# Decay attention in blocks of 64 tokens instead of 128, with a state formed in the middle of each chunk

## The chip, the core and the metric

The kernel runs on one core of a Trainium2 chip. The metric is the device time of one execution in microseconds (us), as the median of repeated runs. Five engines matter here: TensorE (PE, matrix multiplies, which read their weights by a separate load instruction, PEld), VectorE (DVE), ScalarE (ACT), GpSimd (POOL) and SyncE (SP), which issues the DMA transfers. TensorE writes to PSUM, which has eight banks; every tile called "bank" is one of them.

## The reference

Two stages follow each other. The first is linear attention with an exponential decay per head, the second a feed-forward network with a squared ReLU.

```python
B, H, S, D = 4, 8, 768, 64           # q, k, v; lam: one decay per head
# attention, in blocks of 64 tokens:
intra = einsum('bhic,bhjc->bhij', qb, kb) * Dmask      # lam ** (i - j), i >= j
intra = einsum('bhij,bhjd->bhid', intra, vb)
inter = einsum('bhid,bhde->bhie', qb * lam_pow, kv_state)
out   = intra + inter
kv_state = lam_block * kv_state + einsum('bhsd,bhse->bhde', kb * rev_pow, vb)
...
# feed-forward: x is (3072, 512), w_in (512, 2048), w_out (2048, 512)
h = maximum(x @ w_in, 0.0)
result = h * h @ w_out
```

The size of the block is a choice of whoever computes this: a longer block does more of the work as masked scores between tokens, a shorter one does more of it through the state.

## The kernel before, in words

**Tiles and chunks.** The 3072 tokens are cut into 24 chunks of `C = 128` tokens, six for each of four batches. A tile is three chunks (`NT = 3`, 384 columns), so there are eight tiles. For each tile the attention of its three chunks fills the tile's `x` (as a high part `xh` and a low part `xl`), and the feed-forward part then runs 16 steps (`NF`) over the hidden units. A step is `mm1` (L485: 12 multiplies with 384 columns into one bank), the squared ReLU on ACT and DVE (L499 to L506), and `mm2` (L491, L492, L494: 9 multiplies with 512 columns into three banks). From the third tile on, two steps are taken together.

**Attention.** The first chunk of each batch is done by `unit_first`; the change leaves it alone. The 20 others are done by `unit`. A unit has two parts on TensorE:

- `front` (L431): `scores` (L344) multiplies keys with queries, 16 matmuls, then `update` (L350) multiplies decayed keys with values to give what the chunk adds to the state, 16 matmuls. Both write the same two banks `sc`. The last chunk of a batch needs no new state and has only `scores`.
- `both` (L449): the old state is multiplied with the queries (L452, 8 matmuls), and `values` (L358) multiplies the masked scores with the weighted values, 16 matmuls, both into the two banks `ys`.

All these matmuls are 64 by 64 with float32 operands; four of them at a time sit in the four quarters of the array (`QUARTERS`). In `scores` and `values` a chunk is split into two halves of `TW = 64` tokens. Half `j = 0` of the keys meets all 128 queries, half `j = 1` only the 64 later ones, so half of these matmuls have 128 columns and half have 64. The old state meets all 128 queries at once.

**Between the two parts** DVE works. `begin_` (L436) multiplies the scores in `sc` with the mask (L437, two operations over 384 elements), adds the update in `sc` to the old state (L442, two operations over 128 elements, tile `hold`), and scales the new state (L445). After `both`, `back` (L455) copies on ACT (L456), adds and scales on DVE (L457, L458), and splits into `xh` (ACT, L460) and `xl` (DVE, L461).

**What sets the order.** A planner written in Python (`Plan.order`) places every operation on its engine by guessed durations, keys (due times), dependencies and free buffers; its order is what each engine then runs. Guessed durations change the order, not the work. Where the planner expects TensorE to be idle before 45 us it puts in dummy multiplies (`filler`, L230). The first two units, chunks (0,1) and (1,1), are planned alone: `front` and `both` are separate operations of TensorE. The other 18 are fused by `turn_over` (L558): one operation of TensorE holds the `front` of one unit and, behind it, the `both` of the unit before. A fused operation therefore comes about every 20 to 27 us between the steps of the feed-forward part.

**Weights** of the feed-forward part arrive as 64-bit floats and are converted on ACT and DVE (L290 to L300) during roughly the first 110 us.

Of the kernel before, what the change touches and what calls it, by code (L numbers as in the profile page):

```python
# [14 lines left out]
ALU = mybir.AluOpType  # L15
PSUM = bass.MemoryType.PSUM

B, H, S, D = 4, 8, 768, 64
DM, DFF = 512, 2048
P = 128  # L20
C = 128
# [5 lines left out]
R = 2  # L27
# [119 lines left out]
TW = C // 2  # L147
SPAN = C + TW
QUARTERS = ((0, 0), (1, 1), (0, 1), (1, 0))
# [7 lines left out]

TWO, BOTH = 2, 9.0

EDGE = 0.15  # L160

WEIGHTS0, WKEY1, WKEY2, KLATE, ULATE = -9.0, 7.0, 2.0, 6.0, 16.0

LEAD = 0.6


@with_exitstack
def kernel(ctx: ExitStack, tc: tile.TileContext, pn, lamx, w, out):
    nc = tc.nc
# [29 lines left out]
    mask = const.tile([P, 2 * P], F32, name="mask")[:, 0:SPAN]  # L199
# [5 lines left out]
    def at(b):  # L205
        return tiles[b.kind][b.slot]
# [49 lines left out]
    def dm():  # L256
# [6 lines left out]
        out=wd2.rearrange("p (r e) -> p r e", r=R), in0=wdec.rearrange("p (r j e) -> p r j e", r=R, j=2)[:, :, 0],  # L263
        in1=lam[:, 0:H].rearrange("p (r j e) -> p r j e", r=R, j=2)[:, :, 0], op=ALU.mult), [o_pow])
    o = plan.op("PE", 1.0, -12, spread, [o_wb], [wb, dps])
    o_dm = [plan.op("DVE", 0.22, -12, lambda h=h: nc.vector.scalar_tensor_tensor(  # L266
        out=dm()[:, h, 0:C], in0=at(dps)[:, h * C:h * C + C], scalar=wd2[:, h:h + 1], in1=mask[:, 0:C], op0=ALU.mult, op1=ALU.mult), [o, o_wd2], [dps, decay]) for h in range(NS)]
# [3 lines left out]
        out=rdec.rearrange("p (r v) i -> p r v i", v=2)[:, :, v], in0=at(rps[v])[:, 0:2 * C].rearrange("p (r i) -> p r i", r=R),  # L271
        in1=lam[:, H:H + NP].rearrange("p (r v) -> p r v", v=2)[:, :, v].unsqueeze(2).broadcast_to([P, R, C]), op=ALU.mult),
# [40 lines left out]
    half = lambda h: slice(h * 64, h * 64 + 64)  # L313
# [7 lines left out]
    def k_(t, r, s, j):  # L321
        return at(t)[half(r), 0, s * C + j * TW:s * C + j * TW + TW]

    def q_(t, r, s, i=0):
        return at(t)[half(r), 1, s * C + i:s * C + C]

    def head(r, j, e):
        return (r * 2 + j) * 2 + e

    def heads(a):  # L330
        return a.rearrange("p (h d) -> p h d", h=H)
# [7 lines left out]
    def scores(t, sc):  # L339
        for e in range(2):  # L340
            for j in range(2):
                for r, v in QUARTERS:
                    o_ = at(sc[r])[half(v), e * SPAN + j * C:e * SPAN + j * C + C - j * TW]
                    nc.tensor.matmul(o_, k_(t, r, 2 * v + e, j), q_(t, r, 2 * v + e, j * TW), start=e == j == 0, stop=True, skip_group_check=True)  # L344

    def update(kt, vd, u, col, start):
        for e in range(2):
            for j in range(2):
                for v, r in QUARTERS:
                    nc.tensor.matmul(  # L350
                        at(u[v])[half(r), col + e * D:col + e * D + D], kt()[half(v), head(r, j, e)],
                        heads(at(vd))[half(v), head(r, j, e)], start=start and e == j == 0, stop=True, skip_group_check=True)

    def values(v_, s1, ys, start):
        for r in range(R):
            for j in range(2):
                for v, e in QUARTERS:
                    nc.tensor.matmul(  # L358
                        at(ys[v])[half(e), (2 + r) * C + j * TW:(3 + r) * C], v_()[half(v), head(r, j, e)], at(s1[r])[half(v), e, j * C:j * C + C - j * TW],
                        start=start and r == j == 0, stop=j == 1, skip_group_check=True)  # L360

    def y_(ys, v):
        return at(ys[v])[:, 2 * C:4 * C].rearrange("p (r i) -> p r i", r=R)
# [50 lines left out]
    def unit(b, c, x, col, key, span, behind=None, vd_act=False, alone=False):  # L414

        t, tv, vd, s1, xr = Buf("in"), Buf("in"), Buf("half"), [Buf("s1") for _ in range(R)], Buf("half")
        sc, ys = [Buf("bank") for _ in range(2)], [Buf("bank") for _ in range(2)]
        last = c == NC_ - 1
        old, o_old = state[b]

        def add(eng, dur, dk, fn, deps, bufs, name=None):
            o = plan.op(eng, dur, key + dk * span, fn, deps, bufs)
            return in_turn(name, o) if name else o

        i = CHUNKS.index((b, c))
        l = load(1.7, key - 8, lambda: at(t), pn[i, 0], [t], "load", behind)
        loadv = load(1.7, key - 7.9, lambda: at(tv), pn[i, 1], [tv], "load", behind)
        v_, kt = (lambda n=n: heads(at(tv)[:, n]) for n in range(2))
        o_vd = add("ACT" if vd_act else "DVE", 2.2 if vd_act else 0.6, 0, lambda: weighted(v_, vd, vd_act), [loadv, o_pow], [tv, vd], "vd")

        def front():  # L431
            scores(t, sc)
            if not last:
                update(kt, vd, sc, 2 * SPAN, False)

        def begin_(o_sc):  # L436
            so = [add("DVE", 0.45, 0.2, lambda r=r: nc.vector.tensor_tensor(  # L437
                out=at(s1[r]), in0=at(sc[r])[:, 0:2 * SPAN].rearrange("p (e i) -> p e i", e=2),
                in1=mask.unsqueeze(1).broadcast_to([P, 2, SPAN]), op=ALU.mult), [o_sc], [sc[r], s1[r]], f"s1{r}") for r in range(R)]
            if not last:  # L440
                new = Buf("hold")
                os_ = [add("DVE", 0.22, 0.3, lambda v=v: nc.vector.tensor_tensor(  # L442
                    out=at(new)[:, 2 * v:2 * v + 2], in0=at(sc[v])[:, 2 * SPAN:2 * SPAN + 2 * D].rearrange("p (e d) -> p e d", e=2), in1=at(old)[:, 2 * v:2 * v + 2], op=ALU.add),
                    [o_sc] + o_old, [sc[v], new, old]) for v in range(2)]
                state[b] = (new, [add("DVE", 0.35, 0.3, lambda: nc.vector.tensor_tensor(  # L445
                    out=at(new), in0=at(new), in1=lc.unsqueeze(2).broadcast_to([P, NS, D]), op=ALU.mult), os_, [new])])
            return so

        def both():  # L449
            for v in range(2):  # L450
                for r, e in QUARTERS:
                    nc.tensor.matmul(at(ys[r])[half(e), v * C:v * C + C], at(old)[half(r), 2 * v + e], q_(t, r, 2 * v + e), start=v == 0, stop=True, skip_group_check=True)  # L452
            values(lambda: heads(at(vd)), s1, ys, False)

        def back(o_y):  # L455
            oc = [add("ACT", 0.33, 1, lambda r=r: nc.scalar.copy(x4(xr)[:, 2 * r:2 * r + 2], at(ys[r])[:, 0:2 * C].rearrange("p (v i) -> p v i", v=2)), [o_y], [ys[r], xr], f"yi{r}") for r in range(R)]  # L456
            oa = [add("DVE", 0.36, 1, lambda v=v: nc.vector.tensor_tensor(out=by_v(x4(xr), v), in0=y_(ys, v), in1=by_v(x4(xr), v), op=ALU.add), oc, [ys[v], xr]) for v in range(2)]  # L457
            xo = add("DVE", 0.6, 1, lambda: nc.vector.tensor_tensor(out=x4(xr), in0=x4(xr), in1=rdec, op=ALU.mult), oa + o_rdec, [xr])  # L458
            cs = slice(col, col + C)
            oh = add("ACT", 0.55, 1, lambda: nc.scalar.copy(at(x)[0][:, :, cs], x4(xr)), [xo], [xr, x])  # L460
            ol = add("DVE", 0.6, 1, lambda: nc.vector.tensor_tensor(  # L461
                out=at(x)[1][:, :, cs], in0=x4(xr), in1=at(x)[0][:, :, cs], op=ALU.subtract), [oh], [xr, x])
            return [oh, ol]

        dep_f, buf_f, dur_f = [l] + ([] if last else [o_vd, loadv]), [t] + sc + ([] if last else [tv, vd]), 0.7 if last else 1.2
        buf_v, dur_v = ys + [t, vd, x, old] + s1, 1.15
        if alone:
            o_sc = add("PE", dur_f + EDGE, 0, front, dep_f, buf_f, "sc")
            so = begin_(o_sc)
            return back(add("PE", dur_v + EDGE, 1, both, so + [o_vd] + o_old, buf_v, "y"))  # L470
        return dict(key=key, front=Part(dur_f, front, dep_f, buf_f), begin=begin_, values=Part(dur_v, both, [o_vd] + o_old, buf_v), back=back)

    last_mm, steps = {}, {}
# [77 lines left out]
    for f in range(NF):  # L551
        t = FIRST + f * SLOW_STEP
# [35 lines left out]
    def attention(ti):  # L588
        for j, (b, c) in enumerate(TILES[ti]):
            u = unit(b, c, xs[ti], j * C, begin[ti - 1] + (j - LEAD) * NF / NT * per[ti - 1], 4.0, steps[0, BEHIND] if ti == 2 else None)  # L590
            u["last"] = begin[ti - 1] + (NT - LEAD) * NF / NT * per[ti - 1]
            so = turn_over(u)
            pending.append((u, so, done_x[ti]))

    for ti, cs in enumerate(TILES):
        x, ready = xs[ti], done_x[ti]
# [7 lines left out]
        os_ = [Buf("bank") for _ in cs]  # L604
# [44 lines left out]
```

## Time and profile before

| What | Value |
|---|---|
| median of three runs | 611.14 us (611.11 to 611.68) |
| the profiled execution's own time | 611.9 us |
| span of the profiled execution | 610.2 us |
| TensorE matmul records | 5268 |
| VectorE busy over the span | 310.0 us |
| ScalarE busy over the span | 224.8 us |

The profile comes from one execution. A row of a group names line, engine, operation, tiles (output and inputs), shape and count, then busy time in us and the mean of one in ns. A row of the timeline gives start and length in us; neighbouring instructions of one line are merged, with their count behind an x. Every float32 matmul of the program appears as two matmul records: L452 stands in 20 units with 8 matmuls each, and has 320 records. Matmuls overlap one another in the engine, so the length of one record is not the time that it costs; what it costs is read from the starts of successive records or groups.

### The profile page before, as it was taken

To read this page: it belongs to the slowest core of one execution; us is meant where nothing else is said; L and a number is where in the kernel's file an instruction comes from. 1 tells how busy PE (TensorE), PEld (TensorE's weight loads), DVE (VectorE), ACT (ScalarE), POOL (GpSimd) and SP (SyncE) were. 2 spreads that over 40 slices of the span, in tenths; PEclk is the share of its full clock that TensorE was granted. 3 is DMA by queue.
4 is the path that set the end of the run, shared out by engine and by line. 5 is a ranking of instruction groups with operands and counts; after the bars stand their busy time and mean duration, and the time that the engine had idled before them with its cause. 6 is when DMAs were issued, how large, how long until landed. Compare 5 with 4: busy or idle time off the path is not lost.

```text
span 610.2 us, 12175 instructions
## 1 busy us (share of the span) xinstructions
PE 603.4 (99%) x5268; PEld 544.0 (89%) x5268; DVE 310.0 (51%) x623; ACT 224.8 (37%) x477; POOL 4.6 (1%) x14
## 2 busy tenths in 40 slices
PE   8999999999999999999999999999999999999997
PEld 7889999898999898898998998989989899899996
DVE  6899999854334434444353453353443443332222
ACT  6767777542432232232222332322323232232221
POOL 3000000000000000000000000000000000000000
PEclk9999999999999999999999999999999999999999
DMA  8865555532112202112021320130210100010001
GB/s 289 292 217 173 188 193 186 190 127 104 35 53 70 74 32 71 52 36 71 0 71 56 100 70 1 36 110 13 70 48 23 54 1 0 1 37 18 0 1 52
DMA packets 15749, 49.02 MB, mean 80 GB/s; under 512 B 1872, under 2 KB 1872, under 8 KB 15696
## 3 DMA queue, kind: packets, MB, share of 16 engines
q1 hardware_dynamic: 15696, 48.25, 23.6%
q8 instruction: 41, 0.67, 0.5%
q14 instruction: 12, 0.10, 0.1%
HBM read 41.95 MB, written 6.29 MB: 79 GB/s over the span
## 4 chain that ended last, share of the span: by engine, by line
PE 96%; DMA 2%; DVE 1%; ACT 0%; issue 0%; SPq 0%; DVEq 0%
PE bank L485 44%; PE bank L491 15%; PE bank L492 14%; PE bank L494 14%; PE bank L344 3%; PE bank L358 3%; DMA in<-w 2%; PE bank L452 2%; PE bank L350 1%; PE bank L230 1%; DVE in L266 0%; ACT m L290 0%; DVE xl L461 0%; DVE m L540 0%; DVE m L295 0%
## 5 line engine op out<-in xcount | busy, mean ns | idle before, releaser
L491 PE MATMUL bank<-woh,gh 128*128 128x512 f32 x384 | 151.7, 395 | 0.1
L505 DVE TENSOR_TENSOR g<-g 128x384 f32<-128x384 f32 x96 | 53.6, 558 | 190.4 <-ACT gh L504 190.4
L492 PE MATMUL bank<-wol,gh 128*128 128x512 f32 x384 | 149.9, 390 | 0.0
L499 ACT ACTIVATE g<-bank 128x384 f32<-128x384 f32 x128 | 62.8, 491 | 191.2 <-PE bank L485 190.7
L485 PE MATMUL bank<-xh,wih 128*128 128x384 f32 x512 | 110.5, 338 | 0.0
L485 PE MATMUL bank<-xh,wil 128*128 128x384 f32 x512 | 109.6, 336 | 0.0
L485 PE MATMUL bank<-xl,wih 128*128 128x384 f32 x512 | 109.5, 336 | 0.0
L494 PE MATMUL bank<-woh,gl 128*128 128x512 f32 x384 | 100.6, 390 | 0.0
L485 PEld LDWEIGHTS bank<-xh,wih 128*128 128x128 f32 x512 | 91.1, 188 | 4.6
L485 PEld LDWEIGHTS bank<-xh,wil 128*128 128x128 f32 x512 | 90.6, 188 | 0.0
L485 PEld LDWEIGHTS bank<-xl,wih 128*128 128x128 f32 x512 | 90.4, 188 | 0.0
L506 DVE TENSOR_TENSOR gl<-g,gh 128x384 fp32r<-128x384 f32 x128 | 71.4, 558 | 30.7 <-ACT gh L502 21.6
L491 PEld LDWEIGHTS bank<-woh,gh 128*128 128x128 f32 x384 | 72.1, 188 | 14.6 <-ACT gh L502 0.6
L494 PEld LDWEIGHTS bank<-woh,gl 128*128 128x128 f32 x384 | 71.9, 188 | 14.7
L492 PEld LDWEIGHTS bank<-wol,gh 128*128 128x128 f32 x384 | 72.1, 188 | 12.9
L504 ACT ACTIVATE gh<-g 128x384 fp32r<-128x384 f32 x96 | 50.4, 525 | 63.7 <-PE bank L492 61.8
L456 ACT COPY half<-bank 128x256 f32<-128x256 f32 x40 | 12.9, 375 | 50.3 <-PE bank L358 50.3
L290 ACT ACTIVATE m<-in 128x512 f32<-128x512 f32 x32 | 21.5, 675 | 14.2 <-DVE wol L300 6.2
L344 PEld LDWEIGHTS bank<-in 64*64 64x64 f32 x768 | 18.5, 133 | 7.6 <-issue 6.9
L437 DVE TENSOR_TENSOR s<-bank,mask 128x384 f32<-128x384 f32 x40 | 20.6, 552 | 9.1 <-PE bank L350 8.2
L540 DVE COPY ob<-bank 128x512 f32<-128x512 f32 x15 | 10.3, 688 | 23.9 <-PE bank L494 21.1
L297 DVE SCALAR_TENSOR_TENSOR m<-in,m 128x512 uint32<-128x512 uint32 x32 | 22.1, 690 | 0.0
(59 smaller groups left out, 378.5 us busy)
## 6 DMA issues: line engine op xcount, KB each, us to landing
in<-pn SPq DMA_DIRECT2D x44, 512.0 KB, 4.6
in<-w SPq DMA_DIRECT2D x32, 512.0 KB, 3.7
out<-ob SPq DMA_DIRECT2D x23, 256.0 KB, 2.1
half<-pn SPq DMA_DIRECT2D x8, 256.0 KB, 5.5
out<-m SPq DMA_DIRECT2D x1, 256.0 KB, 2.0
g<-lamx SPq DMA_DIRECT2D x1, 8.0 KB, 1.6
```

The costliest lines, as they stand in the source:

```text
L290: o = add("ACT", 0.55, lambda: nc.scalar.activation(at(m), words(1).bitcast(F32), AF.Abs), [o], [st, m])
L297: o = add("DVE", 0.6, lambda: nc.vector.scalar_tensor_tensor(out=bits(), in0=words(0), scalar=29, in1=bits(), op0=ALU.logical_shift_right, ...
L344: nc.tensor.matmul(o_, k_(t, r, 2 * v + e, j), q_(t, r, 2 * v + e, j * TW), start=e == j == 0, stop=True, skip_group_check=True)
L437: so = [add("DVE", 0.45, 0.2, lambda r=r: nc.vector.tensor_tensor(out=at(s1[r]), in0=at(sc[r])[:, 0:2 * SPAN].rearrange("p (e i) -> p e i" ...
L485: nc.tensor.matmul(at(h)[:, 0:N], wt[:, cc, :], xt[:, cc, :], start=k == 0, stop=k == 3 * NCC - 1)
L491: nc.tensor.matmul(at(os_[j]), at(gh)[:, sl], woh[f], start=f == 0, stop=False)
L492: nc.tensor.matmul(at(os_[j]), at(gh)[:, sl], wol[f], start=False, stop=False)
L494: nc.tensor.matmul(at(os_[j]), at(gl)[:, sl], woh[f], start=False, stop=f == NF - 1)
L499: orr = plan.op("ACT", 0.45, key - (AHEAD if ti < 2 else 0), lambda: nc.scalar.activation(at(g), at(h)[:, 0:N], AF.Relu), [o1], [h, turn_, g])
L504: ogh = plan.op("ACT", 0.47, key, lambda: nc.scalar.activation(at(gh), at(g), AF.Square), [orr], [g, gh])
L505: og = plan.op("DVE", 0.48, key, lambda: nc.vector.tensor_tensor(out=at(g), in0=at(g), in1=at(g), op=ALU.mult), [orr, ogh], [g])
L506: ogl = plan.op("DVE", 0.48, key - (AHEAD if ti < 2 else 0), lambda: nc.vector.tensor_tensor(out=at(gl), in0=at(g), in1=at(gh), op=ALU.sub ...
```

## The change

Each chunk of a unit is now treated as two blocks of 64 tokens. A second state, `mid`, is formed for the middle of the chunk: old state plus what the first half adds. The later half of the queries then meets `mid` instead of meeting the first half's keys directly.

- `scores64`: 16 matmuls, all with 64 columns, each half of the keys with its own half of the queries.
- `update64`: 8 matmuls for each half of the chunk, kept apart in the bank. Other chunks have both halves (16 matmuls, as before); the last chunk of a batch, which had none, has the first half (8).
- `old64`: 16 matmuls with 64 columns, the first half of the queries with `old`, the second with `mid`.
- `values64`: 16 matmuls, all with 64 columns.
- On DVE the mask covers 256 elements in each of two operations; two more operations of 128 elements form `mid` in every unit; the new state is then formed from `mid`.
- `front` of a last chunk now also waits for the weighted values and their load, as the other chunks' did.
- The planner's guesses change with it: `EDGE` from 0.15 to 0.2, the mask operation from 0.45 to `S64 = 0.36`, `front` from 1.2 to 1.0 (last chunk 0.7 to 0.75), `both` from 1.15 to 1.0.

```diff
-EDGE = 0.15
+EDGE = 0.2
...
+S64 = 0.36
...
+    def scores64(t, sc):
+        for e in range(2):
+            for j in range(2):
+                for r, v in QUARTERS:
+                    i = (e * 2 + j) * TW
+                    nc.tensor.matmul(at(sc[r])[half(v), i:i + TW], k_(t, r, 2 * v + e, j), q_(t, r, 2 * v + e, j * TW, j * TW + TW), start=e == j == 0, stop=True, skip_group_check=True)
+
+    def update64(kt, vd, u, col, blocks):
+        for j in range(blocks):
+            for e in range(2):
+                for v, r in QUARTERS:
+                    i = col + (j * 2 + e) * D
+                    nc.tensor.matmul(
+                        at(u[v])[half(r), i:i + D], kt()[half(v), head(r, j, e)],
+                        heads(at(vd))[half(v), head(r, j, e)], start=False, stop=True, skip_group_check=True)
+
+    def old64(t, states, ys):
+        for v in range(2):
+            for j in range(2):
+                for r, e in QUARTERS:
+                    i = v * C + j * TW
+                    nc.tensor.matmul(at(ys[r])[half(e), i:i + TW], at(states[j])[half(r), 2 * v + e], q_(t, r, 2 * v + e, j * TW, j * TW + TW), start=v == j == 0, stop=True, skip_group_check=True)
+
+    def values64(vd, s1, ys):
+        for r in range(R):
+            for j in range(2):
+                for v, e in QUARTERS:
+                    i = (2 + r) * C + j * TW
+                    nc.tensor.matmul(
+                        at(ys[v])[half(e), i:i + TW], heads(at(vd))[half(v), head(r, j, e)], s64(s1[r])[half(v), e * 2 + j],
+                        start=False, stop=True, skip_group_check=True)
...
         def front():
-            scores(t, sc)
-            if not last:
-                update(kt, vd, sc, 2 * SPAN, False)
+            scores64(t, sc)
+            update64(kt, vd, sc, 4 * TW, 1 if last else 2)
 
         def begin_(o_sc):
-            so = [add("DVE", 0.45, 0.2, lambda r=r: nc.vector.tensor_tensor(
-                out=at(s1[r]), in0=at(sc[r])[:, 0:2 * SPAN].rearrange("p (e i) -> p e i", e=2),
-                in1=mask.unsqueeze(1).broadcast_to([P, 2, SPAN]), op=ALU.mult), [o_sc], [sc[r], s1[r]], f"s1{r}") for r in range(R)]
+            so = [add("DVE", S64, 0.2, lambda r=r: nc.vector.tensor_tensor(
+                out=s64(s1[r]), in0=at(sc[r])[:, 0:4 * TW].rearrange("p (n i) -> p n i", n=4),
+                in1=mask[:, 0:TW].unsqueeze(1).broadcast_to([P, 4, TW]), op=ALU.mult), [o_sc], [sc[r], s1[r]], f"s1{r}") for r in range(R)]
...
+            om = [add("DVE", 0.22, 0.2, lambda v=v: plus(mid, old, 0, v), [o_sc] + o_old, [sc[v], mid, old]) for v in range(2)]
             if not last:
                 new = Buf("hold")
...
+                os_ = [add("DVE", 0.22, 0.3, lambda v=v: plus(new, mid, 1, v), [om[v]], [sc[v], new, mid]) for v in range(2)]
...
-            return so
+            return so + om
 
         def both():
-            for v in range(2):
-                for r, e in QUARTERS:
-                    nc.tensor.matmul(at(ys[r])[half(e), v * C:v * C + C], at(old)[half(r), 2 * v + e], q_(t, r, 2 * v + e), start=v == 0, stop=True, skip_group_check=True)
-            values(lambda: heads(at(vd)), s1, ys, False)
+            old64(t, states, ys)
+            values64(vd, s1, ys)
...
-        dep_f, buf_f, dur_f = [l] + ([] if last else [o_vd, loadv]), [t] + sc + ([] if last else [tv, vd]), 0.7 if last else 1.2
-        buf_v, dur_v = ys + [t, vd, x, old] + s1, 1.15
+        dep_f, buf_f, dur_f = [l, o_vd, loadv], [t] + sc + [tv, vd], 0.75 if last else 1.0
+        buf_v, dur_v = ys + [t, vd, x, old, mid] + s1, 1.0
```

More of the change, by code (lines that the diff above doesn't have):

```diff
@@ L322, in k_, with q_ @@
         return at(t)[half(r), 0, s * C + j * TW:s * C + j * TW + TW]
-    def q_(t, r, s, i=0):
-        return at(t)[half(r), 1, s * C + i:s * C + C]
+    def q_(t, r, s, i=0, end=C):
+        return at(t)[half(r), 1, s * C + i:s * C + end]
     def head(r, j, e):
@@ L360, in values, with s64 @@
                         start=start and r == j == 0, stop=j == 1, skip_group_check=True)
+    def scores64(t, sc):
[26 more added lines that the diff above has]
+                        start=False, stop=True, skip_group_check=True)
+    def s64(b):
+        return at(b).rearrange("p e i -> p (e i)")[:, 0:4 * TW].rearrange("p (n i) -> p n i", n=4)
     def y_(ys, v):
@@ L429, in unit, with plus @@
         o_vd = add("ACT" if vd_act else "DVE", 2.2 if vd_act else 0.6, 0, lambda: weighted(v_, vd, vd_act), [loadv, o_pow], [tv, vd], "vd")
+        mid = Buf("hold")
+        states = (old, mid)
         def front():
-            scores(t, sc)
-            if not last:
-                update(kt, vd, sc, 2 * SPAN, False)
+            scores64(t, sc)
+            update64(kt, vd, sc, 4 * TW, 1 if last else 2)
         def begin_(o_sc):
-            so = [add("DVE", 0.45, 0.2, lambda r=r: nc.vector.tensor_tensor(
-                out=at(s1[r]), in0=at(sc[r])[:, 0:2 * SPAN].rearrange("p (e i) -> p e i", e=2),
-                in1=mask.unsqueeze(1).broadcast_to([P, 2, SPAN]), op=ALU.mult), [o_sc], [sc[r], s1[r]], f"s1{r}") for r in range(R)]
+            so = [add("DVE", S64, 0.2, lambda r=r: nc.vector.tensor_tensor(
+                out=s64(s1[r]), in0=at(sc[r])[:, 0:4 * TW].rearrange("p (n i) -> p n i", n=4),
+                in1=mask[:, 0:TW].unsqueeze(1).broadcast_to([P, 4, TW]), op=ALU.mult), [o_sc], [sc[r], s1[r]], f"s1{r}") for r in range(R)]
+            def plus(to, base, j, v):
+                i = (4 + 2 * j) * TW
+                return nc.vector.tensor_tensor(
+                    out=at(to)[:, 2 * v:2 * v + 2], in0=at(sc[v])[:, i:i + 2 * D].rearrange("p (e d) -> p e d", e=2), in1=at(base)[:, 2 * v:2 * v + 2], op=ALU.add)
+            om = [add("DVE", 0.22, 0.2, lambda v=v: plus(mid, old, 0, v), [o_sc] + o_old, [sc[v], mid, old]) for v in range(2)]
@@ L440, in begin_ @@
             if not last:
                 new = Buf("hold")
-                os_ = [add("DVE", 0.22, 0.3, lambda v=v: nc.vector.tensor_tensor(
-                    out=at(new)[:, 2 * v:2 * v + 2], in0=at(sc[v])[:, 2 * SPAN:2 * SPAN + 2 * D].rearrange("p (e d) -> p e d", e=2), in1=at(old)[:, 2 * v:2 * v + 2], op=ALU.add),
-                    [o_sc] + o_old, [sc[v], new, old]) for v in range(2)]
+                os_ = [add("DVE", 0.22, 0.3, lambda v=v: plus(new, mid, 1, v), [om[v]], [sc[v], new, mid]) for v in range(2)]
```

## The prediction

> **What bounds the kernel now.** I read the page first, then the busy time by stage, then who waited for whom on TensorE, and last the timeline of single attention blocks.
>
> ```profile
> span 610.2 us, 12175 instructions
> PE 603.4 (99%) x5268; PEld 544.0 (89%) x5268; DVE 310.0 (51%) x623; ACT 224.8 (37%) x477; POOL 4.6 (1%) x14
> PEclk9999999999999999999999999999999999999999
> PE 96%; DMA 2%; DVE 1%; ACT 0%; issue 0%; SPq 0%; DVEq 0%
> ```
>
> TensorE is busy throughout and carries 96% of the chain that ended last, at full granted clock. A busy share says little by itself, because overlapping matmuls count as busy, so I look at it by stage:
>
> ```profile
> core 0: us, PE busy (x) PEld busy (x) DVE busy (x) ACT busy (x) POOL busy (x), PEclk, DMA share, GB/s
> 0.00:16.00 16.00, 13.94 (x262) 11.04 (x262) 10.38 (x29) 9.96 (x34) 4.59 (x14) 1.00 0.84 292
> 16.00:44.00 28.00, 27.49 (x497) 22.93 (x497) 25.64 (x60) 20.71 (x55) 0.00 (x0) 1.00 0.80 268
> 44.00:110.00 66.00, 66.00 (x339) 60.52 (x339) 65.80 (x136) 48.65 (x93) 0.00 (x0) 1.00 0.55 179
> 110.00:527.00 417.00, 417.00 (x3770) 378.07 (x3772) 183.41 (x358) 125.07 (x256) 0.00 (x0) 1.00 0.17 56
> ```
>
> There are three stages. Up to 44 us TensorE has gaps and dummy multiplies and DVE is 92% busy (25.64 of 28). From 44 to 110 us both are full: DVE converts weights, TensorE has a backlog of feed-forward steps. From 110 us on DVE is 44% busy and TensorE has no gap. The waits of TensorE, over the whole span and then from 44 us on (an empty list under its heading), say the same:
>
> ```profile
> PE bank L230 <- DVE ob L213: 1.5, 1, 1.5
> PE bank L358 <- DVE s L391: 0.5, 1, 0.5
> PE bank L452 <- DVE hold L442: 0.4, 1, 0.4
> ```
>
> ```profile
> engine line waited for: us in total, times, longest us
> ```
>
> So behind 44 us every microsecond that TensorE is spared is a microsecond of the result, as long as nothing new makes it wait. All 18 fused units lie there; only the two planned alone lie in the start.
>
> **What a quarter-set of matmuls costs.** Here is a fused block of a normal chunk, and one whose front belongs to the last chunk of a batch. The starts in the first column matter, not the lengths in the second.
>
> ```profile
> 204.67 0.90 PE L344 MATMUL bank<-in 64*64 64x128 f32 x32
> 205.39 0.65 PE L350 MATMUL bank<-half,in 64*64 64x64 f32 x32
> 205.86 0.62 PE L452 MATMUL bank<-in,hold 64*64 64x128 f32 x16
> 206.29 0.85 PE L358 MATMUL bank<-s,half 64*64 64x128 f32 x32
> 207.07 0.50 PE L491 MATMUL bank<-woh,gh 128*128 128x512 f32 x1
> ```
>
> ```profile
> 259.42 0.90 PE L344 MATMUL bank<-in 64*64 64x128 f32 x32
> 260.14 0.62 PE L452 MATMUL bank<-in,hold 64*64 64x128 f32 x16
> 260.57 0.85 PE L358 MATMUL bank<-s,half 64*64 64x128 f32 x32
> 261.35 0.97 PE L485 MATMUL bank<-xh,wih 128*128 128x384 f32 x4
> ```
>
> ```profile
> L344 PE MATMUL bank<-in 64*64 64x128 f32 x384 | 19.1, 282 | 0.0
> L344 PE MATMUL bank<-in 64*64 64x64 f32 x384 | 14.5, 217 | 0.0
> L452 PE MATMUL bank<-in,hold 64*64 64x128 f32 x320 | 12.7, 272 | 0.4 <-DVE hold L442 0.4
> L350 PE MATMUL bank<-half,in 64*64 64x64 f32 x512 | 10.5, 218 | 0.0
> ```
>
> The update is pure 64 columns: 32 records from 205.39 to 205.86, 0.47 us, or eight sets of four at 58 ns (14.7 ns a record). The old-state product is pure 128 columns: 16 records from 205.86 to 206.29, 0.43 to 0.44 us, four sets at 109 ns. The scores are half and half by the form rows, so four sets of each: 4 x 109 + 4 x 58 = 668 ns, and 0.72 us were taken, so 0.05 us is the entry to the block. The values likewise take 0.78 us, 668 ns plus 0.11 us for the way back to the 128-row multiplies. Two prices and two edges explain the whole block, 2.40 us (204.67 to 207.07). A set costs nearly in proportion to its columns, with about 5 ns on top.
>
> **The change on TensorE, part by part**, at 58 ns a set and with the edges unchanged:
> - scores64: eight sets, 464 ns against 668: -0.20 us.
> - update64: normal chunk, the same eight sets: 0. Last chunk, four new sets: +0.23.
> - old64: eight sets, 464 ns against 4 x 109 = 436: +0.03. Twice the matmuls with half the columns each cost only the fixed part.
> - values64: 464 ns against 668: -0.20, so -0.18 for the two parts of `both` together.
>
> A normal unit so saves 0.38 us; a last one 0.20 - 0.23 + 0.18 = 0.15 us. Of the 18 fused units four are last chunks and 14 are not: 14 x 0.38 + 4 x 0.15 = 5.9 us. By the stage table all of it is on the path.
>
> The Trainium skill has a rule against this. The page "TensorE: Matmul & The Clock Gate", section "Wait — 56ns, not 53.3ns?" in Part 1, states that matmuls never start closer than about 25 ns however few columns they have; by that a set of four would cost 100 ns, a normal block 32 x 100 ns and the edges, 3.4 us, and the result would come out some 18 us slower (an estimate from that page). The trace disagrees where it can be read: the update's 32 records start 14.7 ns apart on average, four quarters at work together.
>
> **DVE in a fused block.** Two operations in a row overlap too, so occupancy comes from pairs:
>
> ```profile
> 33.59 0.76 DVE L457 TENSOR_TENSOR half<-bank,half 128x256 f32<-128x256 f32 x2 [0.90 <-ACT half L456]
> 35.80 1.02 DVE L437 TENSOR_TENSOR s<-bank,mask 128x384 f32<-128x384 f32 x2
> 37.76 0.48 DVE L442 TENSOR_TENSOR hold<-bank,hold 128x128 f32<-128x128 f32 x2
> L437 DVE TENSOR_TENSOR s<-bank,mask 128x384 f32<-128x384 f32 x40 | 20.6, 552 | 9.1 <-PE bank L350 8.2
> L442 DVE TENSOR_TENSOR hold<-bank,hold 128x128 f32<-128x128 f32 x32 | 8.7, 283 | 0.0
> L457 DVE TENSOR_TENSOR half<-bank,half 128x256 f32<-128x256 f32 x40 | 15.1, 419 | 13.0 <-ACT half L456 13.0
> ```
>
> A pair's length less one mean is the step: 0.47 us for 384 elements, 0.34 for 256, 0.20 for 128. The mask operations shrink from 384 to 256 elements (-0.26 us a unit), the two that form `mid` add 0.40: +0.14 us a unit. DVE is 44% busy behind 110 us, so it pays this from idle time. Its results are needed a whole unit later by TensorE, since `both` runs one block after its `front`. What does follow soon is the release of the `sc` banks, which now takes one pair more:
>
> ```profile
> 209.34 0.28 DVE L442 TENSOR_TENSOR hold<-bank,hold 128x128 f32<-128x128 f32 x1
> 211.29 0.86 PE L485 MATMUL bank<-xh,wih 128*128 128x384 f32 x4
> ```
>
> The last reader of `sc` ends at 209.62, 1.67 us before the next multiply that opens a bank. With 0.14 us more, or 0.40 if the shorter masks help nothing, 1.2 us are left. I cost it at nothing; without that cover it would be at most 0.40 us a block. In a last chunk `sc` is newly held until `mid` is formed, and its front newly waits for the weighted values; their load is placed a unit ahead, and the planner puts other steps first if they are late.
>
> **The start.** The two units planned alone run before 44 us, where DVE leads.
>
> ```profile
> 38.10 0.75 PE L452 MATMUL bank<-in,hold 64*64 64x128 f32 x13 [0.37 <-DVE hold L442]
> 39.55 1.99 PE L230 MATMUL bank<-ob 128*128 128x256 f32 x8
> 43.83 0.69 DVE L461 TENSOR_TENSOR xl<-half,xh 128x512 fp32r<-128x512 f32 x1
> 44.27 0.86 PE L485 MATMUL bank<-xh,wih 128*128 128x384 f32 x4
> ```
>
> TensorE's endless stretch begins at 44.27, when the second tile's `x` is complete (`xl` at 44.52); just before, it ran dummies for want of DVE. If DVE's occupancy decides, the start moves by 2 x 0.14 = +0.3 us; if the chain through a unit decides, by 2 x (0.14 - 0.38) = -0.5; if TensorE's own work, by -0.8. The new wait for `mid` stands at L452's place in that chain, with the values and the next feed-forward step queued behind it on TensorE. The changed guesses also let the planner reorder DVE's queue, and one conversion operation in the wrong place costs the 0.69 us of a 512-element row such as L461. I take 0, between the ends, since DVE's +0.3 is nearest to what the stage table shows and one unit's shorter chain offsets it; for the range -0.8 to +2 (three misplaced operations).
>
> **Sum.** -5.9 + 0. The profiled execution's own time of 611.9 us (span 610.2 and 1.7 around it) becomes 606.0; the median of the runs, 611.14, lies 0.8 lower and becomes 605.2 us.
>
> **Rivals.**
> 1. *TensorE is limited by the number of records, not by columns* (slower). The update is 32 records in a row; the new block is 128 at that pace, longer than anything the trace holds. Should a queue in front of the array be drained by the short run and refilled more slowly, the block would go at the refill's pace. The block before averages 2.40 us / 112 records = 21.4 ns. At that pace a normal block takes 128 x 21.4 ns = 2.74 us (+0.34, 13 of them), one with a last front, 80 records before (259.42 to 261.35, 1.93 us) and 112 now, 2.40 (+0.47, four), the final values-only block +0.1: +6.4 us, 617.5. It decides from about 18 ns a record, where the 2240 new records cost as much as the old blocks did. Against it: the update comes behind 32 scores records already faster than the block's mean, and shows no slowing. The floor of 25 ns in the Trainium skill (the same page and section) would be its extreme form.
> 2. *New waits in the block.* If banks, or DVE behind a longer queue, hold TensorE for 0.33 us in each of 18 blocks, nothing remains: 611. The margin of 1.67 us and an idle DVE speak against it.
> 3. *The start slips* by 2 to 4 us through another order of DVE's queue: 607.2 to 609.2. The planner is sensitive, and a conversion chain takes several 0.69 us pieces; but the dummies show slack of its own on TensorE only.
> 4. *The change does part of what it says*: sustained sets cost 65 ns instead of 58. 560 sets in the fused blocks x 7 ns = 3.9 us given back: 609.
>
> **How the numbers follow.** Forecast 0.78; rival 1 0.07; rival 2 0.05; rival 3 0.06; rival 4 0.04. The forecast's own range is 604.4 (start at -0.8) to 607.2 (start at +2); to hold 8 in 10 it reaches a little into rivals 3 and 4: 604.2 to 607.8. A measurement of this kernel can tell about 0.2%, 1.2 us, from no change. Faster by more: forecast and rivals 3 and 4, 0.88; within it: rival 2, 0.05; slower: rival 1, 0.07.
>
> **What would show it.** Right: in the profile after, a normal fused block takes 2.02 us from its first record to the next feed-forward multiply, one with a last front 1.79, with sets 58 ns apart in all four groups; TensorE's list of waits behind the start stays empty; matmul records rise by 384 to 5652 less or more a few dummies. Wrong: a block that lengthens after its first 30 to 60 records (rival 1), entries of TensorE waiting for DVE or banks (rival 2), or a first uninterrupted feed-forward step well after 44.3 us (rival 3).

## The result: 606.19 us, and the profile after

The change takes 606.19 us (median of five runs, 605.93 to 608.62) beside 611.56 us for the kernel before (five runs). The ratio is 0.9922, with a 95% interval from 0.9909 to 0.9935. The forecast was 605.2 us, with a range of 604.2 to 607.8. The profiled execution took 605.93 us, where 606.0 was worked out for it. In a later comparison the same kernel took 606.28 us (four runs) beside 611.52 us (eleven): 0.9916, interval 0.9900 to 0.9931.

The page of the profile after shows the same picture as before, 6.0 us shorter, with 388 matmul records more (384 from the change and two more dummy multiplies, which have two records each):

```profile
span 604.2 us, 12989 instructions
PE 598.2 (99%) x5656; PEld 538.5 (89%) x5656; DVE 312.0 (52%) x663; ACT 225.0 (37%) x477; POOL 4.7 (1%) x14
PE 94%; DMA 3%; ACT 1%; DVE 1%; issue 0%; SPq 0%; ACTq 0%; DVEq 0%
```

The busy time by stage (last stage cut where the attention ends) still has TensorE without a gap behind 44 us, and DVE at 45% behind 110 us:

```profile
44.00:110.00 66.00, 66.00 (x340) 60.45 (x339) 65.92 (x137) 49.15 (x93) 0.00 (x0) 1.00 0.57 181
110.00:521.00 411.00, 411.00 (x4091) 372.10 (x4093) 184.42 (x392) 124.78 (x256) 0.00 (x0) 1.00 0.17 57
```

Whom TensorE waited for: two entries in all, both in the start. From 44.4 us on the list is empty.

```profile
PE bank L232 <- DVE ob L215: 1.5, 1, 1.5
PE bank L385 <- DVE hold L482: 0.3, 1, 0.3
```

The timeline of TensorE shows the fused block of a normal chunk, and one with a last chunk's front (L369 scores, L376 update, L385 old state, L392 values):

```profile
203.42 0.69 PE L369 MATMUL bank<-in 64*64 64x64 f32 x32
203.94 0.65 PE L376 MATMUL bank<-half,in 64*64 64x64 f32 x32
204.40 0.65 PE L385 MATMUL bank<-in,hold 64*64 64x64 f32 x32
204.87 0.65 PE L392 MATMUL bank<-s,half 64*64 64x64 f32 x32
205.45 0.50 PE L533 MATMUL bank<-woh,gh 128*128 128x512 f32 x1
...
257.42 0.69 PE L369 MATMUL bank<-in 64*64 64x64 f32 x32
257.94 0.41 PE L376 MATMUL bank<-half,in 64*64 64x64 f32 x16
258.17 0.65 PE L385 MATMUL bank<-in,hold 64*64 64x64 f32 x32
258.64 0.65 PE L392 MATMUL bank<-s,half 64*64 64x64 f32 x32
259.21 0.45 PE L527 MATMUL bank<-xh,wih 128*128 128x384 f32 x1
```

Read the starts again: 0.52, 0.46, 0.47 and 0.58 us, 2.03 in all where 2.40 stood. The block with a last front takes 1.79 us where 1.93 stood.

For the whole, take the stretch from the second tile's first feed-forward multiply to the last multiply of the kernel. The first pair of rows is the kernel before (its start stands in the prediction already), the second the change:

```profile
605.59 0.39 PE L494 MATMUL bank<-woh,gl 128*128 128x512 f32 x1
```

```profile
44.53 0.86 PE L527 MATMUL bank<-xh,wih 128*128 128x384 f32 x4
600.03 0.39 PE L536 MATMUL bank<-woh,gl 128*128 128x512 f32 x1
```

Before it is 605.59 - 44.27 = 561.32 us, after it 600.03 - 44.53 = 555.50: 5.82 us saved. The stretch began 0.26 us later, and what follows the last multiply (output and end of the program) took 4.2 us instead of 4.6. Together that is the 6.0 us between the spans.

All of the 5.82 us can be found in the blocks. From 100 us on there are 19 fused operations of TensorE: 13 normal blocks, four with a last chunk's front, one with a front alone (1.29 us before, 1.09 after) and one with `both` alone (1.26 and 1.09). Each taken from its first record to the next feed-forward multiply, they add up to 41.52 us before and 35.67 us after: 5.85 us.

### The profile page after: what moved, and what is told of

Same layout as the page of the kernel before. It is cut to its first block, busy times and chain, and to the rows that moved or that the text cites. A ratio compares the mean times of both kernels' runs of the same rounds, so it can differ in the third digit from the quotient of the medians.

```text
span 604.2 us, 12989 instructions
## 1 busy us (share of the span) xinstructions
PE 598.2 (99%) x5656; PEld 538.5 (89%) x5656; DVE 312.0 (52%) x663; ACT 225.0 (37%) x477; POOL 4.7 (1%) x14
## 4 chain that ended last, share of the span: by engine, by line
PE 94%; DMA 3%; ACT 1%; DVE 1%; issue 0%; SPq 0%; ACTq 0%; DVEq 0%
PE bank L527 43%; PE bank L533 15%; PE bank L534 14%; PE bank L536 14%; PE bank L369 2%; DMA in<-pn 2%; PE bank L385 1%; DMA in<-w 1%; PE bank L392 1%; PE bank L376 1%; ACT half L405 1%; PE bank L232 1%; PE bank L360 0%; PE bank L346 0%; ACT m L292 0%
## 5 line engine op out<-in xcount | busy, mean ns | idle before, releaser
L527 PE MATMUL bank<-xh,wih 128*128 128x384 f32 x512 | 110.6, 338 | 0.0
L527 PE MATMUL bank<-xh,wil 128*128 128x384 f32 x512 | 109.6, 336 | 0.0
L527 PE MATMUL bank<-xl,wih 128*128 128x384 f32 x512 | 109.5, 336 | 0.0
L527 PEld LDWEIGHTS bank<-xh,wih 128*128 128x128 f32 x512 | 91.2, 188 | 4.6
L527 PEld LDWEIGHTS bank<-xh,wil 128*128 128x128 f32 x512 | 90.6, 188 | 0.0
L527 PEld LDWEIGHTS bank<-xl,wih 128*128 128x128 f32 x512 | 90.4, 188 | 0.0
L498 ACT COPY half<-bank 128x256 f32<-128x256 f32 x40 | 12.9, 374 | 46.5 <-PE bank L392 46.5
L299 DVE SCALAR_TENSOR_TENSOR m<-in,m 128x512 uint32<-128x512 uint32 x32 | 21.8, 682 | 0.1
L297 DVE SCALAR_TENSOR_TENSOR m<-in,m 128x512 uint32<-128x512 uint32 x32 | 21.8, 683 | 0.1
L407 DVE TENSOR_TENSOR half<-in,tables 128x512 f32<-128x512 f32 x18 | 12.4, 691 | 18.2 <-DMA in<-pn 18.2
```

The lines of the kernel that those rows point to most:

```text
L297: o = add("DVE", 0.6, lambda: nc.vector.scalar_tensor_tensor(out=bits(), in0=words(1), scalar=0xC0000000, in1=bits(), op0=ALU.bitwise_and, ...
L299: o = add("DVE", 0.6, lambda: nc.vector.scalar_tensor_tensor(out=bits(), in0=words(0), scalar=29, in1=bits(), op0=ALU.logical_shift_right, ...
L527: nc.tensor.matmul(at(h)[:, 0:N], wt[:, cc, :], xt[:, cc, :], start=k == 0, stop=k == 3 * NCC - 1)
```

## The experiments

### Where the time sits: order, start and work

Is the gain the work or the order? This kernel has the change's work and the old guesses of the planner.

```diff
-EDGE = 0.2
+EDGE = 0.15
-S64 = 0.36
+S64 = 0.45
...
-..., 0.75 if last else 1.0
+..., 0.7 if last else 1.2
-buf_v, dur_v = ys + [t, vd, x, old, mid] + s1, 1.0
+buf_v, dur_v = ys + [t, vd, x, old, mid] + s1, 1.15
```

> The change, but with the planner's guesses of before (EDGE 0.15, mask operation 0.45, front 1.2 and 0.7, both parts behind it 1.15). The work on the engines is that of the change; only the order and the number of dummy multiplies can differ. Theory (columns): blocks of 2.02 and 1.79 us again; the time moves only by what the start moves, within 1 us of the change: 605.5 to 607.2. Rival (the guesses made the gain): 609 to 611.5.

It ran beside the unchanged change:

> The change as it is, timed beside the variants of it on one chip. Theory (columns set the price of a matmul on TensorE, and all fused blocks are on the path): about 606.2 us, with normal fused blocks of 2.02 to 2.03 us and a first long stretch of feed-forward steps from about 44.5 us. Rival (the gain came from another order of the work): no other number here; it is told apart by the kernel with the old guesses.

Two more variants asked what the start lost to DVE. One leaves out the forming of the middle state:

```diff
-            om = [add("DVE", 0.22, 0.2, lambda v=v: plus(mid, old, 0, v), ...
+            om = [add("DVE", 0.22, 0.2, lambda: None, ...
-        states = (old, mid)
+        states = (old, old)
-            ... plus(new, mid, 1, v)
+            ... plus(new, old, 1, v)
```

> The change without the two DVE operations that form the middle state; the planner still reserves their time, so each engine keeps its order. What is left out: the middle state is not computed, both halves of the queries meet the old state, and the new state lacks the first half's part. Theory: the change lost 0.26 us at the start to DVE's extra work (two units, two operations of 0.20 us each, less the shorter masks) and nothing later. So the feed-forward stretch begins 0.2 to 0.8 us earlier (44.53 back to 43.7 to 44.3), the fused blocks stay at 2.02 us, and the time is 605.4 to 606.0. Rival (forming the state also holds up the fused blocks): 2 us or more below the change. Second rival (the start is set by TensorE or the planned order alone): the same time as the change within 0.1 us.

The other gives the two units planned alone their old form:

```diff
         if alone:
-            o_sc = add("PE", dur_f + EDGE, 0, front, dep_f, buf_f, "sc")
+            o_sc = add("PE", 1.35, 0, front128, dep_f, buf_f, "sc")
...
```

`front128`, and `begin128` and `both128` behind it, are `front`, `begin_` and `both` of the kernel before.

> The change for the 18 fused units, the form of before (blocks of 128, with its guesses) for the two units that are planned alone in the start, where DVE leads. Theory: the start goes back to that of the kernel before, the feed-forward stretch begins at about 44.27 instead of 44.53 us, and the time is 0.26 us below the change, about 605.9 us. Rival (the 0.26 us are chance of the planner's order, or the hardware's spread): the same as the change within 0.1 us, or later.

After these four, two profiles were taken to see whether the start repeats. The kernel before:

> The kernel before once more, for the start and the stretch behind it. Theory (the stretch from the second tile's first feed-forward multiply to the last multiply is fixed by TensorE's work; where it begins differs from run to run with the landing of the first weights and chunks): stretch 561.3 us within 0.1, its beginning anywhere between 43.5 and 47 us. Rival (the start belongs to the kernel's order): it begins at 44.28 us within 0.1 again.

And the variant with the old form in the start:

> The variant with blocks of 128 in the two units planned alone, once more. Theory (start by the landing of transfers): stretch 555.5 us within 0.1, beginning anywhere between 43.5 and 47 us, so not at 46.82 again. Rival (this order of the start is later by its own nature): 46.8 us within 0.2 again.

Each kernel's median is from its timed runs; start, end and stretch are from the timeline of its profiled execution, read as above.

| Kernel | Median us | Stretch begins | Last multiply | Stretch us |
|---|---|---|---|---|
| before | 611.52 | 44.27 | 605.59 | 561.32 |
| before, again | one run, 611.07 | 43.38 | 604.74 | 561.36 |
| the change | 606.19 | 44.53 | 600.03 | 555.50 |
| the change, again | 606.28 | 46.03 | 601.55 | 555.52 |
| old guesses | 605.79 | 43.55 | 599.01 | 555.46 |
| no middle state | 607.59 | 46.15 | 601.63 | 555.48 |
| old form in the start | 605.29 | 46.81 | 602.59 | 555.78 |
| the same, again | one run, 605.72 | 43.92 | 599.83 | 555.91 |

The stretch repeats within 0.04 us for one kernel's order of work and within 0.13 for the last variant. It is 5.8 us shorter with the new blocks under either set of guesses (5.4 to 5.6 in the variant whose start has the old form, and whose order differs too), and forming the middle state adds nothing to it (555.50 and 555.52 with, 555.48 without). The old guesses do give VectorE another order, from its 49th operation on. The fused operations add up to 35.67 us in all six profiles with the new form behind the start. So the gain is TensorE's work in the fused blocks; the rival of a better order falls.

Where the stretch begins is another matter. It moved by 1.5 us between two executions of the same kernel, and by 2.9 us in the last variant. ScalarE's rows show what moved with it in three executions; the bracket holds its wait for a transfer. First the change, then the change again, then the old form in the start:

```profile
36.99 0.68 ACT L292 ACTIVATE m<-in 128x512 f32<-128x512 f32 x1 [1.39 <-DMA in<-w]
```

```profile
38.48 0.69 ACT L292 ACTIVATE m<-in 128x512 f32<-128x512 f32 x1 [2.24 <-DMA in<-w]
```

```profile
32.66 2.02 ACT L405 ACTIVATE half<-in,tables 128x64 f32<-128x64 f32 x8 [2.60 <-DMA in<-pn]
```

The first weights and chunks land at different times. That the start follows them is argued from such rows, not tested; the variant without the middle state had a late wait of this kind too (2.77 us, before the row at 38.59) and began at 46.15. In the last of the three executions something else was added: from 35.9 to 39.3 us TensorE was granted only half its clock (0.50). My reading that the change loses 0.26 us there to DVE is neither shown nor refuted: leaving the two operations out gave a stretch that began at 46.15 and not at 43.7 to 44.3 as expected, and the variant that should have been 0.26 us faster began once at 46.81 and once at 43.92. Its median of 605.29 us (604.62 to 608.5) and the old guesses' 605.79 (604.9 to 607.24) overlap with the change's 606.01 to 607.46; none of them is a version that can be said to beat it. Five of the six times of the old form, 604.62 to 606.01, lie at or below the lowest of the change there, so the start may well cost something; the sixth, 608.5, is above all of the change's.

### What a set of four costs, and how long a run may be

Each kernel of this part and the next was timed once, beside 610.93 or 610.97 us for the kernel before. The first cuts each 64-column matmul into two of 32 columns (here in the scores; the other three groups alike):

```diff
             for j in range(2):
+              for n in range(0, TW, TW // 2):
                 for r, v in QUARTERS:
-                    i = (e * 2 + j) * TW
-                    nc.tensor.matmul(at(sc[r])[half(v), i:i + TW], ..., q_(t, r, 2 * v + e, j * TW, j * TW + TW), ...
+                        i = (e * 2 + j) * TW + n
+                        nc.tensor.matmul(at(sc[r])[half(v), i:i + TW // 2], ..., q_(t, r, 2 * v + e, j * TW + n, j * TW + n + TW // 2), ...
```

> Every 64-column matmul of the 20 units is cut into two of 32 columns, one set of four after the other: twice the records, the same columns, and each of the weights loaded twice. Theory (columns, with about 5 ns a set on top): a set takes 26.7 + 5 = 32 ns, a normal block 64 sets and 0.16 us of edges, 2.2 us, and the whole 609 us. Rival (at 64 columns it is already the record or its weight load that sets the pace, so that the next halving buys nothing): 58 ns a set, a normal block of 3.9 us, 560 more sets in the fused blocks, 638 to 640 us.

It took 668.19 us, more than either. The timeline of two of its normal blocks shows two effects:

```profile
449.80 1.14 PE L370 MATMUL bank<-in 64*64 64x32 f32 x64
450.75 1.11 PE L378 MATMUL bank<-half,in 64*64 64x32 f32 x64
451.69 1.11 PE L388 MATMUL bank<-in,hold 64*64 64x32 f32 x64
452.62 1.11 PE L396 MATMUL bank<-s,half 64*64 64x32 f32 x64
453.67 0.50 PE L537 MATMUL bank<-woh,gh 128*128 128x512 f32 x1
...
392.60 1.11 PE L388 MATMUL bank<-in,hold 64*64 64x32 f32 x64
393.54 0.76 PE L396 MATMUL bank<-s,half 64*64 64x32 f32 x39
395.94 0.59 PE L396 MATMUL bank<-s,half 64*64 64x32 f32 x25 [1.65 <-issue]
396.46 0.50 PE L537 MATMUL bank<-woh,gh 128*128 128x512 f32 x1
```

The first block is free of stops: 64 records of 32 columns take 0.93 us, 58 ns a set, just what a set of 64 columns takes. My step "nearly in proportion to its columns, with about 5 ns on top" is wrong below 64 columns. In the second block TensorE stops in the midst of a run, and the profile shows nothing that it waits for ("issue"). Of the 62 us by which this kernel is slower than the change, its dearer sets are 32 us (the blocks without their stops add up to 67.9 us, against 35.67) and its stops 18 us. Up to 8 us more (an estimate: 0.04 of 190 us) went between 110 and 300 us, where TensorE's granted clock was 0.96. To separate the two effects, two kernels lengthen the run and leave the columns alone:

```diff
         def front():
-            scores64(t, sc)
+            for _ in range(1 if alone else 5):
+                scores64(t, sc)
```

> In the 18 fused units the 16 score matmuls are issued five times over (the same products into the same places). A normal block holds 256 records in a row instead of 128, 512 instructions with the weight loads. Theory (columns): each repeat takes 0.467 us, a normal block 2.03 + 4 x 0.467 = 3.89 us, 18 fronts make 33.6 us, 640 us in all; the last score record of a block is as near to its neighbour as the first. Rival (a queue in front of the array feeds the run and is refilled more slowly, at the 21 ns a record of the rivals' reckoning): the block lengthens after its first 60 to 130 records, to 4.4 us or more, 648 us and above.

The second has 3 in the place of 5:

> The score matmuls three times over in the 18 fused units: a normal block holds 192 records in a row (384 instructions with the weight loads), between the change's 128 and the 256 of the longer run. Theory, formed from the longer run (every stop there lies at the same place modulo 256 TensorE instructions, 16 KB of them, and never before record 150 of a run): instructions come in pieces of 256, the next piece is there when the run begins, and the one after it takes longer than the 1.87 us in which 128 records use up a piece. So only a run with two such borders well inside it stops. A run of 192 records has the second border inside it in some of the blocks: 4 to 9 of the 18 stop once for 1.1 to 1.9 us, all between records 140 and 192, at the same remainder, the rest keep 58 ns a set (2.96 us a normal block); 628 to 638 us in all. Rival (the pace itself falls after so many records): every block is longer, at the same record. Second rival (the stops need 256 records): none, 623 us.

Five times took 661.55 us, three times 630.58. Here are two normal blocks of the longer run, a clean one and one that stops, and then the waits of TensorE in the shorter run (columns: us in total, times, longest):

```profile
384.76 2.56 PE L369 MATMUL bank<-in 64*64 64x64 f32 x160
387.14 0.65 PE L376 MATMUL bank<-half,in 64*64 64x64 f32 x32
387.61 0.65 PE L385 MATMUL bank<-in,hold 64*64 64x64 f32 x32
388.07 0.65 PE L392 MATMUL bank<-s,half 64*64 64x64 f32 x32
388.65 0.50 PE L534 MATMUL bank<-woh,gh 128*128 128x512 f32 x1
...
200.41 0.65 PE L385 MATMUL bank<-in,hold 64*64 64x64 f32 x32
200.87 0.40 PE L392 MATMUL bank<-s,half 64*64 64x64 f32 x13
202.59 0.56 PE L392 MATMUL bank<-s,half 64*64 64x64 f32 x19 [1.31 <-issue]
203.08 0.50 PE L534 MATMUL bank<-woh,gh 128*128 128x512 f32 x1
```

```profile
PE bank L392 <- issue: 2.9, 2, 1.5
PE bank L385 <- issue: 2.4, 2, 1.2
```

The clean block takes 3.89 us, to the hundredth what eight sets at 58 ns for each repeat give: the pace does not fall with the length of a run, so that part of rival 1 is refuted. But most runs of 256 records stop, once, for 1.1 to 1.9 us (from one start to the next). Fourteen blocks of the longer run stop, twelve of the 32-column kernel, and four of the shorter run, as expected of it. In the longer run the stops cost 20 us; without them 640 us were expected, and 661.55 were measured. If one counts the matmul records from the start of the program up to each of these 30 stops, doubles the count for the weight loads and divides by 256, the remainder lies between 166 and 176 for all of them, and all come at record 153 of their run or later.

Three other stops belong to the same series. One of 0.28 us comes at record 146 in the shorter run (remainder 174). Two come in the start of the 32-column kernel, where runs of 128 records follow each other 4 us apart: a wait of 1.64 us five multiplies behind one such run, and one of 0.43 us at record 121 of the next (remainder 182 for both).

So the stops point to instructions that arrive in pieces of 256 and run out. This row counts the instruction transfers:

```profile
q8 instruction: 44, 0.72, 0.5%
```

It is from the profile of the change: 0.72 MB in 44 transfers of 16 KB (41 in the kernel before). At 256 instructions to a transfer, 44 make 11264, where TensorE has 11312 records of matmuls and weight loads; 41 make 10496, where it has 10536. The times fit as well: each of the 30 stops ended 1.2 to 1.6 us after such a transfer had landed, and that transfer had begun inside the run. At 14.6 ns a record a run uses up a piece in 128 x 14.6 = 1.87 us, and in these runs the next one was not there by then. A border in the first ten records of a run did no harm: for two such runs of the shorter kernel, at 394.06 and 469.38 us, the transfer had landed 1.7 to 1.8 us before the run began. The Trainium skill agrees on the pieces: the page "Runtime: NRT & Kernel Launch", section "Instruction fetch mechanics", has instructions streamed in 16 KiB blocks while the current one runs. It calls the cost mostly hidden, and there the trace differs where a run of short matmuls holds two borders, 128 records apart, and the first is not at its very beginning. The change's own run, 128 records, is just short enough that no block stopped.

The last kernel of this part asks what holds a set at 58 ns: it cuts the weights of the score matmuls into two times 32 columns and keeps 64 moving columns.

```diff
             for j in range(2):
+              for m in range(0, TW, TW // 2):
                 for r, v in QUARTERS:
-                    nc.tensor.matmul(at(sc[r])[half(v), i:i + TW], k_(t, r, 2 * v + e, j), ...
+                    nc.tensor.matmul(at(sc[r])[slice(v * 64 + m, v * 64 + m + 32), i:i + TW], k_(t, r, 2 * v + e, j)[:, m:m + 32], ...
```

> In the 20 units each of the 16 score matmuls is cut into two by its weights: two records pairs with 32 columns of weights each and the same 64 moving columns, in different strips of the array. The other groups stay. Theory A (at 64 columns and below, a set of four is limited by the number of records, 14 ns each): the score group of 64 records takes 0.95 us as it did with 32 moving columns, and the kernel about 614 us. Theory B (it is limited by the columns of weights that are loaded): half the weights a record, so 0.52 us as in the change, and about 606 us.

It took 615.68 us, some 3 us of it two more stops, at records 152 and 154 of runs that are 160 records long here. The start of the score group (in the window from 205.79 to 205.95 us), and the whole group:

```profile
205.71 0.45 PE L370 MATMUL bank<-in 64*32 64x64 f32 x32
```

```profile
205.71 0.86 PE L370 MATMUL bank<-in 64*32 64x64 f32 x64
206.49 0.69 PE L377 MATMUL bank<-half,in 64*64 64x64 f32 x32
```

Neither theory's number came out: the group took 0.78 us, between 0.52 and 0.95. But its first 32 records took 0.45 us less the 0.22 of the last one's own length, 7 ns a record. A floor of 14 ns for a record (theory A) is refuted by that. With 64 columns of weights four records take 58 ns, at 64 or at 32 moving columns; with 32 columns of weights eight take about that in the first half of the group. That points to the loading of the weights, but does not show it: the narrower weights also lie in eight strips of the array instead of four quarters, and a fixed time for each place would give the same. The single starts show where the rest of the 0.78 us went: a pause of 0.08 us in the middle of the group, about 10 ns a record behind it, and 0.15 us from its last record to the first of the update. Why stays open.

### How much DVE may do behind a block

The mask operations of the fused units were issued seven and thirteen times:

```diff
-            so = [add("DVE", S64, 0.2, lambda r=r: nc.vector.tensor_tensor(...), [o_sc], ...
+            so = [add("DVE", S64, 0.2, lambda r=r: [nc.vector.tensor_tensor(...) for _ in range(1 if alone else 7)], [o_sc], ...
```

> In the 18 fused units each of the two mask operations is issued seven times: 12 more operations of 0.34 us, 4.1 us of DVE directly behind each front, with the planner's order as in the change. Theory, mended after looking at the order of the banks: the bank of the scores is opened again only by the fourth multiply of a feed-forward step behind the block, and that of the values by the second, 4.7 us after DVE has read it; so 4.1 us more are still covered and the time is 606 to 608 us. Rival (the margin as the prediction read it, 1.2 to 1.7 us, is the cover): TensorE waits about 2.5 us in each of 18 blocks, 650 us.

> As with seven mask operations, but thirteen: 24 more operations of 0.34 us, 8.2 us of DVE behind each front. Theory (cover of 4.7 us up to the second step that follows): TensorE waits about 3.4 us in each normal block and less where a block is followed by other work, 635 to 670 us, and its waits are named as waits for DVE's reading of the values' banks. Rival (DVE in the fused part is hidden whatever it does): 606 to 608 us.

Seven took 626.85 us, thirteen 758.12. The waits of TensorE, first with seven, then with thirteen:

```profile
PE bank L527 <- DVE hold L482: 4.9, 1, 4.9
PE bank L527 <- DVE half L499: 4.3, 2, 2.6
PE bank L527 <- DVE ob L582: 2.0, 1, 2.0
```

```profile
PE bank L527 <- DVE half L499: 71.0, 13, 8.1
PE bank L527 <- DVE hold L482: 24.2, 4, 9.9
```

Both expectations were too low, yet the mechanism is the one named: a feed-forward multiply (L527) waits for DVE to be done with a bank. With seven, 4.1 us more of DVE stayed covered behind 14 of the 18 fronts; four such waits remain, all before 186 us. In the planner's order the first four blocks have one of their banks opened again 2.7 to 4.1 us later by its own times, the others 6.2 us or more. Of the 20.7 us by which this kernel is slower than the change, TensorE's waits behind 110 us are 12.9; the granted clock of 0.90 between 110 and 160 us may be some 5 more (an estimate, 0.10 of 50 us). From 190 to 530 us TensorE had no gap at all. The rival with 2.5 us in each of 18 blocks fails. With thirteen, nearly every block waits, 5.5 us on average where 3.4 were expected, and the clock falls with it, as the stages show (the column behind the engines is the granted clock):

```profile
0.00:110.00 110.00, 105.55 (x1117) 92.43 (x1118) 100.97 (x225) 78.18 (x178) 4.68 (x14) 1.00 0.65 216
110.00:200.00 90.00, 66.14 (x686) 58.41 (x685) 61.23 (x141) 24.65 (x51) 0.00 (x0) 0.85 0.21 70
200.00:650.00 450.00, 372.98 (x3301) 336.46 (x3299) 295.25 (x668) 94.53 (x196) 0.00 (x0) 0.89 0.11 39
```

While TensorE waits so often, its granted clock is 0.85 to 0.89 instead of 1.00.

## Why the prediction was right

**The bound.** Right. All that TensorE was spared in the blocks, 5.85 us, came out in the stretch behind 44 us: 5.8 us in the change, under its own guesses and the old ones.

**The terms of the sum.** Right to about 0.01 us each: scores -0.20 (0.72 to 0.52), update -0.01 (0.47 to 0.46), old state +0.04 (0.43 to 0.47), values -0.20 (0.78 to 0.58); a last front's block 1.79 us as worked out. 5.9 us were forecast for the fused units, 5.8 measured.

**The reason behind the price of a set** held for 128 and 64 columns and is wrong as a rule. Half of the 109 ns of a 128-column set is 54.5 ns, so at 64 columns the price by columns and the floor of 58 ns that the 32-column kernel shows lie nearly on top of one another. The prediction took its price from rows of 64 columns, the size of the change, and so came out right in spite of the rule; the "5 ns on top" gave 32 ns for a 32-column set, where 58 were measured.

**DVE and the banks.** Costing it at nothing was right: no wait of TensorE behind 44.4 us. The margin was misread. The multiply at 211.29 that I took for the one to reopen the scores' bank opens another, as the planner's order of the banks shows: there, and behind 13 of the 18 fronts of the change, a bank of the scores comes round only with the fourth feed-forward step behind the block. The cover was larger there than the 1.2 us that I left. Behind the first front the first step opens it, and behind the second front and three of the last chunks' fronts the second; with thirteen mask operations the waits for `hold` (L482), the last reader of the scores' bank, came behind the first front and those three.

**The start.** I took 0 between -0.8 and +2. The profile has +0.26, but the start of one kernel differs more than that between executions, so no sign can be given to this term. Between the forecast of 605.2 and the median of 606.19 lies 1 us. About 0.4 us of it is that the 611.14 the forecast set out from was a median of three runs, where five gave 611.56 and later eleven 611.52. The rest is that the medians lie 5.4 us apart (4.0 to 5.6 by the interval), and not 5.9; 5.8 us in the stretch is a little more than that. The starts of the timed runs would have to account for the difference, which was not shown run by run.

**Rivals.** 1, many records: the pace does not fall, but a supply of instructions that runs short is real, and bites in longer runs than the change's. 2, new waits: none; it takes DVE work of several us more. 3, a slipping start: seen as scatter; with one or two profiles of each order, an effect of the order can't be told from it. 4, sets of 65 ns: refuted at 58.

## What to carry to other kernels

Price small matmuls by the starts of whole sets that work in different quarters of the array, never by the length of a record, and read the price at the very size that the change will use: going from 128 to 64 columns halved the cost of a set here, from 64 to 32 it saved nothing. Keep an unbroken run of such matmuls at or below 128 records with their loads, with long matmuls between two runs. The change's blocks of 128 records, 7 us apart and more, never stopped; two of 13 with 160 records did, and so did runs of 128 that stood 4 us apart in the start of the 32-column kernel. Where the start of a kernel scatters by more than the effect in question, compare the stretch that the bound engine works through without a gap; it repeated to 0.04 us for one order, where single runs scattered by 1 to 3.

## What the runs showed of the hardware

TensorE can run out of instructions: single stops of 1.1 to 1.9 us in runs of 160 records and more, always between 166 and 176 modulo 256 instructions, each ended 1.2 to 1.6 us after an instruction transfer of 16 KB had landed. With weights of 64 columns a set of four takes 58 ns at 64 and at 32 moving columns; with weights of 32 columns records came 7 ns apart in the first half of a group. And a TensorE that waits 5 us in each of some 18 places loses clock as well, down to 0.85 in a stage. Shorter stops can go with it too, but need not: the 32-column kernel had 0.96 between 110 and 300 us, the longer run, with as many stops, 1.00.
